# A decode step of two attention and two gated feed-forward layers: one PSUM bank of scores for a group's 4096 keys, 64 KB loads of K and V

## The chip, the cores and the metric

One of the eight cores of a Trainium2 chip runs the kernel. The metric is the device time of one execution in microseconds (us). The trace comes from one execution under the hardware profiler. TensorE's granted clock is shown in tenths of 2.4 GHz.

## The reference, cut to what matters

```python
B, Sq, D = 4, 1, 512;  Hq, Hkv, Sk, Dh = 32, 8, 4096, 128;  F = 1792      # all float32
def A(x, k_cache, v_cache, wq, wo):             # k_cache, v_cache: [B, Hkv, Sk, Dh]
    q = (x @ wq).reshape(B, Sq, Hq, Dh).transpose(0, 2, 1, 3)
    k, v = repeat(k_cache, 4, axis=1), repeat(v_cache, 4, axis=1)
    p = softmax(einsum("bhqd,bhkd->bhqk", q, k) * Dh ** -0.5)
    return einsum("bhqk,bhkd->bhqd", p, v).transpose(0, 2, 1, 3).reshape(B, Sq, Hq * Dh) @ wo
def Bff(x, w1, w3, w2):
    return (silu(x @ w1) * (x @ w3)) @ w2
for _ in range(2):                              # both layers use the same caches and weights
    x = x + A(layernorm(x), k_cache, v_cache, wq, wo)
    x = x + Bff(layernorm(x), w1, w3, w2)
```

K and V are 67.1 MB each and are needed in both layers; the buffer on the chip holds a small part of them.

## The kernel before

Everything streams from the device's memory on one queue, that of SyncE (SP). A host step lays the arrays out so that each load is 128 partitions by one contiguous row. Sizes are given per partition: 1 KB is 131,072 bytes.

Work goes by group: one of the 8 K/V heads, with its 4 query heads and all 4 batch rows. A group's 4096 keys are done in 4 steps of 1024 keys (SC). A step's K is one 16 KB row per partition and so is its V; `cache` (L92) splits some into 8 and 4 KB loads near the start and at the layers' ends. `score` (L292) makes two PSUM tiles of scores in 256-column products, four at a time, one for each batch row in its 32 output partitions. `maximum` (L312) keeps a running maximum over the steps and `sums` (L334) and the ends of `weigh` (L348) rescale the running sums (an online softmax). `turn` (L326) transposes the exponents, 128 columns at a time, and `weigh` multiplies them with V in 128-column products with 4 weight columns each. The steps are software-pipelined: `finish` (L447) of one step runs behind `score` of the next. x is kept as rows of a [128, 128] tile and is transposed for each projection (`layernorm`, L240). `busy` (L225) issues filler transposes on TensorE at eight places outside the attention steps; their counts stand in BUSY.

The order of the loads is written out in `plan` (L121 to L146). `pump` (L150) issues the next loads as long as `take` finds contiguous room; `done` and `vacate` give room back when the last product that needs a load has been issued, and pump again. So SP waits, load by load, for the products that free its room. There are three homes: the pool (96 KB), wq_sb (64 KB) and wo_sb (56 KB); in layer 1 the room of wq and wo is given to the stream as their groups are used. Layer 1 goes through the groups in reverse. K of group 7 (TURN), which ends layer 0, stays for layer 1: 60 KB in the pool and the last 4 KB in two PSUM banks (`stored`), from where ScalarE copies it back. wo's first group has no home of its own and is loaded in each layer.

Of the kernel before, what the change touches and what calls it, by code (L numbers as in the profile page):

```python
# [28 lines left out]
POOL = 96  # L29


TURN = HKV - 1
STORED = (STEPS - 1, 3)
W2_PARTS = ((0, 4), (4, 8), (8, 12), (12, 13), (13, 14))
BUSY = (5, 3, 5, 3, 3, 7, 3, 4)
SCRATCH = 1024

# [3 lines left out]
def tile_decode_layers(ctx: ExitStack, tc: tile.TileContext, x, kt, v, wq, wo, w1, w3, w2, out):  # L43
# [17 lines left out]

    homes = {"pool": pool, "wq": wq_sb.rearrange("p g k n -> p (g k n)"),
             "wo": wo_sb.rearrange("p g h e -> p (g h e)")}
    free = [("pool", 0, POOL)]

    def take(n):
        for i, (home, at, size) in enumerate(free):
            if size >= n:
                free[i:i + 1] = [(home, at + n, size - n)] if size > n else []
                return home, at, n  # L70
        return None

    def give(home, at, n):
        for other in list(free):
            if other[0] == home and other[1] + other[2] == at:
                free.remove(other)
                at, n = other[1], other[2] + n
            elif other[0] == home and at + n == other[1]:
                free.remove(other)
                n += other[2]  # L80
        free.append((home, at, n))

# [3 lines left out]
    def stream(keys, src):  # L86
        plan.append((keys, src, None))

    def keep(dst, src):
        plan.append((None, src, dst))  # L90

    def cache(which, layer, i, g, c):  # L92
        src = (kt if which == "k" else v)[g, c]
        last = i == len(orders[layer]) - 1
        if which == "k" and (g, c) == (TURN, STORED[0]):
            parts = (2, 1, 1)
        elif last:
            parts = (2, 1, 1)
        elif layer == 0 and i == 0:
            parts = (1, 1, 2)  # L100
        elif which == "v" and ((layer == 0 and i >= len(orders[0]) - 3) or (layer and i < 2)):
            parts = (2, 2)
        else:
            parts = (4,)
        r = 0
        for n in parts:
            keys = [(which, layer, g, c, r + j) for j in range(n)]
            if which == "k" and g == TURN and layer:
                if (c, r) == STORED:
                    stream(keys, None)  # L110
            else:
                stream(keys, src[:, r * U:(r + n) * U])
            r += n

    def wq_load(a, b):
        keep(wq_sb[:, a:b].rearrange("p g k n -> p (g k n)"), wq[:, a * 2 * U:b * 2 * U])

    def wo_load(a, b):
        keep(wo_sb[:, a - 1:b - 1].rearrange("p g h e -> p (g h e)"), wo[:, a * 2 * U:b * 2 * U])

    for layer in range(LAYERS):  # L121
        steps = orders[layer]
        if layer == 0:
            wq_load(0, 1)
        for i, (g, c) in enumerate(steps):
            cache("k", layer, i, g, c)
            if layer == 0 and c == 1 and g in (0, 1, 3, 5):
                wq_load(*{0: (1, 2), 1: (2, 4), 3: (4, 6), 5: (6, 8)}[g])
            if i:
                cache("v", layer, i - 1, *steps[i - 1])  # L130
            if layer == 0 and c == 2:
                if g == 0:
                    stream([("wo", 0)], wo[:, 0:2 * U])
                elif g in (1, 3, 5):
                    wo_load(g, g + 2)
        cache("v", layer, len(steps) - 1, *steps[-1])
        if layer == 0:
            wo_load(TURN, HKV)
        else:
            stream([("wo", 1)], wo[:, 0:2 * U])  # L140
        for name, w in (("w1", w1), ("w3", w3)):
            for k in range(KC):
                stream([(name, layer, k)], w[:, k * F:(k + 1) * F])
        for i, (a, b) in enumerate(W2_PARTS):
            stream([("w2", layer, i)], w2[:, a * D:b * D])

    state = {"next": 0}
    where, left, room = {}, {}, {}

    def pump():  # L150
        while state["next"] < len(plan):
            keys, src, dst = plan[state["next"]]
            if keys is None:
                nc.sync.dma_start(dst, src)
            else:
                width = U if src is None else src.shape[-1]
                got = take(width // KB)
                if got is None:
                    return
                dst = homes[got[0]][:, got[1] * KB:got[1] * KB + width]  # L160
                if src is None:
                    for i in range(2):
                        nc.scalar.activation(dst[:, i * U // 2:(i + 1) * U // 2], stored[i], AF.Copy)
                else:
                    nc.sync.dma_start(dst, src)
                n = width // len(keys)
                left[state["next"]] = len(keys)
                room[state["next"]] = got
                for i, key in enumerate(keys):
                    where[key] = dst[:, i * n:(i + 1) * n], state["next"]  # L170
                    if key[:3] == ("k", 0, TURN) and key[3:] != STORED:
                        where["k", 1, *key[2:]] = where[key]
                        kept.add(key)
            state["next"] += 1

    kept = set()

    def loaded(*key):
        return where[key][0]

    def done(*key):
        if key in kept:
            return
        i = where[key][1]
        left[i] -= 1
        if left[i] == 0:
            give(*room[i])
            pump()

    def vacate(home, at, n):  # L190
        give(home, at, n)
        pump()

    x_sb = const.tile([P, P], F32, name="x_sb")
    nc.scalar.dma_start(x_sb, x)
    pump()

# [3 lines left out]
    same = const.tile([P, 32], F32, name="same")  # L201
    nc.vector.tensor_reduce(same, ident.rearrange("p (k c) -> p c k", k=4), axis=AX.X, op=ALU.add)
    nc.vector.tensor_scalar(same, same, 1.0 / D, None, op0=ALU.mult)
    spare = const.tile([P, 1], F32, name="spare")
    half = const.tile([P, 1], F32, name="half")
    nc.vector.memset(half, -0.5)
    qT = const.tile([P, B, 32], F32, name="qT")
    nc.vector.memset(qT, 0.0)
    oT = const.tile([P, REP, B], F32, name="oT")
    hT = const.tile([P, 14, B], F32, name="hT")  # L210
    sums_ps = psum.tile([P, 2, P], F32, name="sums_ps")
    nc.vector.memset(sums_ps, 0.0)
# [314 lines left out]
```

## Time and profile before

| | |
|---|---|
| median of 3 runs | 727.63 us (726.88 to 729.59) |
| span of the profiled execution, first to last instruction | 725.7 us |
| what lies around the span, against the median | 1.9 us |
| TensorE, VectorE, ScalarE busy | 474.8, 195.1, 120.2 us |
| moved by DMA | 301.20 MB, 415 GB/s over the span |
| mean granted TensorE clock | 0.882 |

The page gives no time of the profiled execution apart from its span, so the span is what a sum is made against. Busy shares are means over the whole span; the page's rows of 40 slices (18.1 us each) show when something was busy. In a timeline each row is a start, a duration, an engine and a line; `x8` merges eight instructions. A float32 product is two MATMUL instructions with a weight load each, a transpose is one. A DMA row is the time that SP needs to issue it, not its transfer.

### The profile page before, as it was taken

How to read it: one execution, taken by the hardware profiler on the slowest of the kernel's cores; microseconds unless marked ns; L12 is line 12 of the kernel's file. 1: busy time of each engine (PE TensorE's matmuls, PEld its weight loads, DVE VectorE, ACT ScalarE, POOL GpSimd, SP SyncE). 2: the span in 40 equal slices, each digit the busy share in tenths (PEclk: the TensorE clock that was granted, in tenths of full speed). 3: DMA queues.
4: the chain of work that ended last, by engine and by line, in shares of the span. 5: the costliest groups of instructions: out<-in, count | busy, mean ns of one | idle time of the engine just before them, and what ended most of it. 6: DMA issues, size and time to landing. Idle time of an engine off the chain costs nothing.

```text
span 725.7 us, 18239 instructions
## 1 busy us (share of the span) xinstructions
PE 474.8 (65%) x8246; PEld 298.8 (41%) x8246; DVE 195.1 (27%) x694; ACT 120.2 (17%) x323; POOL 2.9 (0%) x10
## 2 busy tenths in 40 slices
PE   5664576744766556666667885666766657666687
PEld 3342344523444334444425554444444434443444
DVE  2122123221323113223202342223222233222220
ACT  1111111111111111111310221111111111111120
POOL 0000000000000000000000000000000000000000
PEclk9687878888988679999989999898989998998788
DMA  9999999999999999999989999999999999999995
GB/s 364 429 426 425 426 427 426 425 427 427 427 424 426 430 425 426 425 426 419 416 356 391 378 429 424 428 427 425 425 426 427 425 427 426 426 426 424 417 418 228
DMA packets 25853, 301.20 MB, mean 415 GB/s; under 512 B 2864, under 2 KB 3120, under 8 KB 7216
## 3 DMA queue, kind: packets, MB, share of 16 engines
q1 hardware_dynamic: 25632, 299.97, 98.4%
q8 instruction: 65, 1.06, 0.6%
q14 instruction: 12, 0.10, 0.0%
q10 hardware_dynamic: 144, 0.07, 0.0%
HBM read 299.96 MB, written 0.07 MB: 413 GB/s over the span
## 4 chain that ended last, share of the span: by engine, by line
DMA 86%; PE 12%; DVE 1%; issue 1%; SPq 0%; ACT 0%; ACTq 0%; DVEq 0%
DMA pool<-in_v 45%; DMA pool<-in_kt 21%; DMA wo_sb<-in_v 6%; DMA wq_sb<-in_v 5%; PE sums_ps L353 4%; DMA pool<-in_w 4%; PE scores L303 3%; DMA pool<-in_wo 2%; DMA wo_sb<-in_w 2%; PE turned L329 1%; PE scores L229 1%; PE scores L396 1%; PE sums_ps L425 1%; DVE stat L306 0%; PE misc L269 0%
## 5 line engine op out<-in xcount | busy, mean ns | idle before, releaser
L353 PE MATMUL sums_ps<-pool,pT 128*4 128x128 f32 x3552 | 143.1, 303 | 132.2 <-DMA pool<-in_v 107.6
L353 PEld LDWEIGHTS sums_ps<-pool,pT 128*4 128x4 f32 x3552 | 91.5, 93 | 171.2 <-issue 101.2
L303 PE MATMUL scores<-pool,qT 128*32 128x256 f32 x1760 | 118.3, 413 | 58.2 <-DMA pool<-in_kt 52.7
L323 ACT ACTIVATE p<-scores,stat 128x512 f32<-128x512 f32 x128 | 87.0, 680 | 270.9 <-PE turned L329 210.7
L306 DVE TENSOR_REDUCE stat<-scores 128x1 f32<-128x512 f32 x128 | 88.5, 691 | 135.2 <-PE scores L303 135.2
L303 PEld LDWEIGHTS scores<-pool,qT 128*32 128x32 f32 x1760 | 62.2, 117 | 97.1 <-issue 68.5
L329 PE MATMUL turned<-ident,p 128*128 128x128 f32 x512 | 96.2, 317 | 0.0
L331 DVE COPY pT<-turned 128x64 f32<-128x64 f32 x128 | 28.1, 220 | 239.2 <-PE turned L329 238.8
L329 PEld LDWEIGHTS turned<-ident,p 128*128 128x128 f32 x512 | 61.8, 157 | 47.3 <-issue 45.6
L318 ACT ACTIVATE stat<-stat 128x1 f32<-128x1 f32 x48 | 14.1, 295 | 266.0 <-DVE stat L316 266.0
L269 PE MATMUL misc<-wq_sb,xT 128*32 128x128 f32 x512 | 25.2, 302 | 0.7 <-DVE ve L258 0.4
L323 ACT ACTIVATION_READ_ACCUMULATOR p<-scores,stat 128x1 f32 x128 | 24.5, 192 | 0.0
L229 PE MATMUL scores<-ident 128*128 128x128 f32 x104 | 19.2, 315 | 1.4 <-POOL ident masks.py:199 1.4
L380 PE MATMUL sums_ps<-wo_sb,oT 128*4 128x128 f32 x448 | 15.6, 282 | 6.1 <-DVE o L362 5.4
L353 PE MATMUL sums_ps<-wq_sb,pT 128*4 128x128 f32 x320 | 11.9, 288 | 9.3 <-DMA wq_sb<-in_v 7.7
L269 PEld LDWEIGHTS misc<-wq_sb,xT 128*32 128x32 f32 x512 | 17.0, 123 | 1.5 <-ACT xT L251 0.4
L303 PE MATMUL scores<-wq_sb,qT 128*32 128x256 f32 x176 | 14.0, 466 | 3.5 <-DMA wq_sb<-in_kt 3.5
L353 PE MATMUL sums_ps<-wo_sb,pT 128*4 128x128 f32 x224 | 10.1, 337 | 9.3 <-DMA wo_sb<-in_v 8.1
L229 PEld LDWEIGHTS scores<-ident 128*128 128x128 f32 x104 | 12.9, 158 | 7.3 <-issue 5.3
L380 PEld LDWEIGHTS sums_ps<-wo_sb,oT 128*4 128x4 f32 x448 | 10.8, 88 | 11.3 <-DVE o L362 9.8
L364 DVE SCALAR_TENSOR_TENSOR o<-o,stat,sums_ps 128x128 f32<-128x128 f32 x32 | 11.0, 343 | 15.5 <-PE sums_ps L353 15.5
L396 PE MATMUL scores<-pool,xT 128*32 128x448 f32 x64 | 9.8, 700 | 5.6 <-DMA pool<-in_w 5.6
(81 smaller groups left out, 185.3 us busy)
## 6 DMA issues: line engine op xcount, KB each, us to landing
pool<-in_kt SPq DMA_DIRECT2D x49, 2048.0 KB, 29.5
pool<-in_v SPq DMA_DIRECT2D x49, 2048.0 KB, 29.3
pool<-in_v SPq DMA_DIRECT2D x10, 1024.0 KB, 14.6
wq_sb<-in_kt SPq DMA_DIRECT2D x5, 2048.0 KB, 37.7
wq_sb<-in_v SPq DMA_DIRECT2D x5, 2048.0 KB, 39.1
pool<-in_w SPq DMA_DIRECT2D x8, 896.0 KB, 9.0
wq_sb<-in_w SPq DMA_DIRECT2D x7, 896.0 KB, 17.1
wq_sb<-in_wq SPq DMA_DIRECT2D x3, 2048.0 KB, 32.5
```

The source lines that it names most:

```text
L229: nc.tensor.transpose(pt[:, 0:P], ident, ident)
L269: nc.tensor.matmul(pq[32 * h:32 * h + 32, 0, :], xT[:, 32 * k:32 * k + 32], wq_sb[:, g, k, h * DH:(h + 1) * DH], start=(k == 0), stop=(k = ...
L303: nc.tensor.matmul(ps[32 * b:32 * b + 32, r * QC:(r + 1) * QC], qT[:, b, :], t[:, b, :], start=True, stop=True)
L306: nc.vector.tensor_reduce(st["stat"][:, h:h + 1], ps, axis=AX.X, op=ALU.max, negate=True)
L318: nc.scalar.activation(stat[:, 6:7], stat[:, 2:3], AF.Exp, bias=stat[:, 3:4], scale=-1.0)
L323: nc.scalar.activation(st["p"].rearrange("p n s -> p (n s)"), st["ps"][h], AF.Exp, bias=stat[:, 3:4], accum_out=stat[:, 4 + h:5 + h])
L329: nc.tensor.transpose(pt[:, n, :], st["p"][:, n, :], ident)
L331: nc.vector.tensor_copy(pT, pt.rearrange("p n (b h) -> p n b h", b=B)[:, :, :, 0:REP])
L353: nc.tensor.matmul(o_ps[32 * b:32 * b + REP, :], st["pT"][h][:, NT * (r % 2) + n, b, :], t[:, b, n, :], start=(r == 0 and n == 0), stop=(r ...
L364: nc.vector.scalar_tensor_tensor(acc["o"], acc["o"], st["stat"][:, 6:7], o_ps, op0=ALU.mult, op1=ALU.add)
L380: nc.tensor.matmul(x_ps[32 * k:32 * k + B, :], oT[:, h, :], w[:, h, k * P:(k + 1) * P], start=(h == 0), stop=(h == REP - 1))
L396: nc.tensor.matmul(ps[32 * j:32 * j + 32, 0:FJ], xT[:, 32 * k:32 * k + 32], w[:, j * FJ:(j + 1) * FJ], start=(k == 0), stop=(k == KC - 1))
```

## The change

A group's K is one load of 64 KB per partition and so is its V. `scores` accumulates all 8 blocks of 512 keys into one PSUM bank: the query sits in a padded tile (`qpad`), and a block's products take the 32 columns of it in which the group's four heads stand in the rows of that block, so that row 4 blk + h of a batch row's 32 holds head h of block blk. One maximum, one exponent, and a factor for each row (in `softmax`: two 32-by-32 transposes on VectorE, a few small operations and an exponent) take the place of the running maximum. `weigh` multiplies four blocks of V side by side (512 columns) with all 32 rows and picks the matching parts with `sel`. x is kept turned (`xT`, [128, 4, 4]), so projections need no transpose ahead of them, and their outputs are turned back by products with a selection matrix (`rows`). The filler transposes are gone. One arena of 213 KB has wq at 0 to 64, wo at 64 to 128 and the kept V of group 7 at 128 to 192 (all K and V streams use 64 to 213 in layer 0). wo is loaded once, after the last V of layer 0, and all its products with layer 0's outputs follow there.

```diff
+NB = 8;  BK = SK // NB;  NI = BK // P;  GW = SK * B;  WT = 14;  ARENA = 213        # KB = 256 columns
+    WQ, WO, KEPT = 0, 64, 128
+    free = [(WO, ARENA - WO)]                        # take: first fit; a load at < WO has its own place
+    load(wq[:, 0:8 * KB], 8, [("wq", 0, 0)], WQ)     # a load: source, KB per key, keys, place
+    for n in range(HKV):
+        cache("k", 0, n, (32, 32) if n == 0 else (64,))
+        if n == 0:
+            load(wq[:, 8 * KB:64 * KB], 8, [("wq", 0, g) for g in range(1, HKV)], WQ + 8)
+        else:
+            cache("v", 0, n - 1, (64,))
+    cache("v", 0, TURN, (32, 16, 8, 8))              # at KEPT; not loaded again in layer 1
+    weights("wo", wo, 0, (32, 16, 8, 8), 8, WO)
+    for name, w in (("w1", w1), ("w3", w3)):
+        weights(name, w, 0, (7, 7, 7, 7), 7)
+    weights("w2", w2, 0, (6, 6, 6, 6, 2, 2), 2)
+    cache("k", 1, TURN, (8,) * 8)
+    for n in range(1, HKV):
+        cache("k", 1, order[1][n], (16,) * 4 if n == 1 else (64,))
+        if n > 1:
+            cache("v", 1, order[1][n - 1], (64,))
+    cache("v", 1, 0, (32, 16, 16))
+    for name, w in (("w1", w1), ("w3", w3)):
+        weights(name, w, 1, (28,), 7)
+    weights("w2", w2, 1, (16, 8, 2, 2), 2)
...
+    def project_q(layer, g, rq, ps):
+        w = loaded("wq", 0, g).rearrange("p (k n) -> p k n", k=KC)
         for k in range(KC):
+            nc.tensor.matmul(ps[32 * k:32 * k + 32, :], xc[:, k, :], w[:, k, :], start=True, stop=True)
+        if layer:
+            vacate("wq", 0, g)
+        yield
+        nc.vector.tensor_scalar(t, ps, rq(), None, op0=ALU.mult)
+        m = misc()
+        for h in range(REP):
+            nc.tensor.matmul(m[:, h, :], t[:, h * P:(h + 1) * P], rows[:, 0:B], start=True, stop=True)
+        nc.vector.tensor_copy(qT[:, g], m)
+        yield
+    def scores(layer, g, pieces=iter(())):
+        for blk in range(NB):
+            k = loaded("k", layer, g, blk).rearrange("p (b s) -> p b s", b=B)
+            lo = PAD - REP * blk
+            for b in range(B):
+                nc.tensor.matmul(s_ps[32 * b:32 * b + 32, :], qpad[:, b, lo:lo + 32], k[:, b, :],
+                                 start=(blk == 0), stop=(blk == NB - 1))
+            done("k", layer, g, blk)
+            next(pieces, None)
+    def softmax():
+        nc.vector.tensor_reduce(top[:, 0:1], s_ps, axis=AX.X, op=ALU.max, negate=True)
+        l = small("l")
+        nc.scalar.activation(p, s_ps, AF.Exp, bias=top[:, 0:1], accum_out=l)
...
+        return {"parts": parts, "sums": sums}
+    def turn_p(st):
+        for i in range(NI):
+            nc.tensor.transpose(t_ps[:, i, :], p[:, i * P:(i + 1) * P], ident)
+        nc.vector.tensor_copy(pT.rearrange("p i r -> p (i r)"), t_ps.rearrange("p i r -> p (i r)"))
+        m = total(st["sums"])
...
+    def weigh(layer, g, st, pieces=iter(())):
+        for f in range(2):
+            for i in range(NI):
+                key = ("v", 0 if g == TURN else layer, g, NI * f + i)
+                w = loaded(*key).rearrange("p (b n) -> p b n", b=B)
+                for b in range(B):
+                    nc.tensor.matmul(o_ps[32 * b:32 * b + 32, :], pT[:, i, 32 * b:32 * b + 32], w[:, b, :],
+                                     start=(i == 0), stop=(i == NI - 1))
+                if g != TURN or layer:
+                    done(*key)
+                yield
+            next(pieces, None)
+            if f == 0:
+                nc.scalar.activation(t, o_ps, AF.Copy, scale=st["parts"][:, 0:1])
+            else:
+                nc.vector.scalar_tensor_tensor(t, o_ps, st["parts"][:, 1:2], t, op0=ALU.mult, op1=ALU.add)
+        m = misc()
+        for j in range(4):
+            nc.tensor.matmul(flat(m), t[:, j * P:(j + 1) * P], sel[:, j].rearrange("p h b -> p (h b)"),
+                             start=(j == 0), stop=(j == 3))
+        nc.vector.tensor_tensor(oT[:, g].rearrange("p h b -> p (h b)"), flat(m), st["r"], op=ALU.mult)
+    def project_o(layer, g, first, last):            # 4 products of 512 columns; layer 1 vacates wo's group
...
+    def collect():
+        nc.vector.tensor_copy(t, x_ps)
+        m = misc()
+        for k in range(KC):
+            nc.tensor.matmul(m[:, k, :], t[:, k * P:(k + 1) * P], rows[:, 0:B], start=True, stop=True)
+        nc.vector.tensor_tensor(xT, xT, m, op=ALU.add)
...
+    def rest_of(qs):
+        for i in range(1, HKV):
+            run(qs[i])
+            if i + 2 < HKV:
+                next(qs[i + 2])
+            yield
...
+        center()                                     # mean by one product with 1/512, then subtract
+        banks = (q_ps, o_ps, t_ps.rearrange("p i r -> p (i r)")) if layer else (q_ps,)
+        for q in qs[:len(banks)]:
+            next(q)
+        nc.vector.tensor_scalar(scale["q"], deviation(), SCALE, None, op0=ALU.mult)
+        run(qs[0])
+        place_q(steps[0])
+        for n, g in enumerate(steps):
+            if layer == 0:
+                scores(layer, g)
+                ahead = qs[n + 1] if n + 1 < HKV else iter(())
+                next(ahead, None)
+                st = softmax()
+                if before is not None:
+                    run(weigh(layer, *before, ahead))
+                run(ahead)
+            else:
+                if n == 0:
+                    scores(layer, g, rest_of(qs))
+                elif n == 1:
+                    heavy = weigh(layer, *before)
+                    scores(layer, g, zip(heavy, heavy))
+                    run(heavy)
+                else:
+                    scores(layer, g)
+                st = softmax()
+                if n > 1:
+                    run(weigh(layer, *before))
+                if n:
+                    project_o(layer, before[0], n == 1, False)
+            if n + 1 < HKV:
+                place_q(steps[n + 1])
+            turn_p(st)
+            before = (g, st)
```

The feed-forward keeps its products (448 columns for w1 and w3); w2 is 14 products of 512 columns in layer 0 and 56 of 128 in layer 1, where x itself is added by four more products into the same bank.

## Rows read from the trace of the kernel before

**Rows 1.** The page: shares, slices, DMA totals.
```profile
PE 474.8 (65%) x8246; PEld 298.8 (41%) x8246; DVE 195.1 (27%) x694; ACT 120.2 (17%) x323; POOL 2.9 (0%) x10
...
PEclk9687878888988679999989999898989998998788
...
GB/s 364 429 426 425 426 427 426 425 427 427 427 424 426 430 425 426 425 426 419 416 356 391 378 429 424 428 427 425 425 426 427 425 427 426 426 426 424 417 418 228
DMA packets 25853, 301.20 MB, mean 415 GB/s; under 512 B 2864, under 2 KB 3120, under 8 KB 7216
...
q1 hardware_dynamic: 25632, 299.97, 98.4%
q8 instruction: 65, 1.06, 0.6%
```

**Rows 2.** The page: the chain that ended last, by engine.
```profile
DMA 86%; PE 12%; DVE 1%; issue 1%; SPq 0%; ACT 0%; ACTq 0%; DVEq 0%
```

**Rows 3.** Timeline of SP in layer 1: start, us, issues.
```profile
513.19 0.33 SPq L165 DMA_DIRECT2D wo_sb<-in_kt  x1
518.08 0.33 SPq L165 DMA_DIRECT2D pool<-in_v  x1
522.97 0.33 SPq L165 DMA_DIRECT2D pool<-in_kt  x1
527.86 0.33 SPq L165 DMA_DIRECT2D pool<-in_v  x1
533.27 0.33 SPq L165 DMA_DIRECT2D pool<-in_kt  x1
...
646.77 0.33 SPq L165 DMA_DIRECT2D wq_sb<-in_kt  x1
```

**Rows 4.** Timeline, layer 0's feed-forward: w1's last, w3's last, w2's first products.
```profile
371.35 0.96 PE L396 MATMUL scores<-pool,xT 128*32 128x448 f32 x8 [1.20 <-DMA pool<-in_w]
...
380.05 1.72 PE L396 MATMUL scores<-pool,xT 128*32 128x448 f32 x8 [0.42 <-DMA pool<-in_w]
...
383.86 1.06 PE L425 MATMUL sums_ps<-pool,hT 128*4 128x128 f32 x32
```

**Rows 5.** Windows: busy times, granted clock (PEclk), DMA share, GB/s.
```profile
core 0: us, PE busy (x) PEld busy (x) DVE busy (x) ACT busy (x) POOL busy (x), PEclk, DMA share, GB/s
376.00:377.00 1.00, 1.00 (x8) 0.00 (x0) 0.00 (x0) 0.00 (x0) 0.00 (x0) 0.50 0.96 401
413.00:680.00 267.00, 181.90 (x3326) 118.19 (x3318) 80.34 (x284) 46.68 (x132) 0.00 (x0) 0.90 1.01 426
```

**Rows 6.** Chain of waits: 16 score products of 256 columns.
```profile
42.11 3.68 PE scores L303 x32
...
406.06 1.77 PE scores L303 x32
```

**Rows 7.** Timeline: weight loads of transposes.
```profile
342.17 0.43 PEld L329 LDWEIGHTS turned<-ident,p 128*128 128x128 f32 x4 [0.41 <-issue]
...
715.54 0.66 PEld L411 LDWEIGHTS turned<-ident,gate 128*128 128x128 f32 x3
```

**Rows 8.** Groups by form.
```profile
L306 DVE TENSOR_REDUCE stat<-scores 128x1 f32<-128x512 f32 x128 | 88.5, 691 | 135.2 <-PE scores L303 135.2
L323 ACT ACTIVATE p<-scores,stat 128x512 f32<-128x512 f32 x128 | 87.0, 680 | 270.9 <-PE turned L329 210.7 <-issue 48.0 <-DVE stat L316 12.3
...
L269 PE MATMUL misc<-wq_sb,xT 128*32 128x128 f32 x512 | 25.2, 302 | 0.7 <-DVE ve L258 0.4 <-issue 0.3
...
L260 POOL TENSOR_TENSOR rstd<-ve,half 128x1 f32<-128x1 f32 x4 | 2.2, 550 | 698.8 <-DVE ve L258 698.8
```

**Rows 9.** The end: timeline, windows, DMA issues.
```profile
712.55 1.72 PE L396 MATMUL scores<-wo_sb,xT 128*32 128x448 f32 x8 [0.43 <-DMA wo_sb<-in_w]
...
722.73 0.29 DVE L429 SCALAR_TENSOR_TENSOR x_sb<-sums_ps,x_sb 128x128 f32<-128x128 f32 x1 [5.21 <-PE sums_ps L425]
...
723.06 0.35 SPq L487 DMA_DIRECT2D out<-x_sb  x1
...
714.00:715.00 1.00, 1.00 (x8) 0.80 (x5) 0.66 (x1) 0.00 (x0) 0.00 (x0) 0.50 0.75 307
720.00:721.00 1.00, 1.00 (x24) 0.82 (x28) 0.00 (x0) 0.00 (x0) 0.00 (x0) 1.00 0.18 53
721.00:722.00 1.00, 1.00 (x24) 0.65 (x15) 0.00 (x0) 0.00 (x0) 0.00 (x0) 1.00 0.00 0
...
out<-x_sb SPq DMA_DIRECT2D x1, 64.0 KB, 1.5
```

More of the change, by code (lines that the diff above doesn't have):

```diff
@@ L62, in tile_decode_layers @@
[L62 to L70, printed above, removed]
-        return None
[L73 to L81, printed above, removed]
@@ L84, in tile_decode_layers @@
-    plan = []
[L86 to L104, printed above, removed]
+    arena = const.tile([P, ARENA * KB], F32, name="arena")
@@ L105, in cache, with load @@
+    plan = []
+    def load(src, per, keys, at=None):
+        plan.append((src, per, keys, at))
+    def cache(which, layer, g, parts):
+        src = (kt if which == "k" else v)[g]
         r = 0
         for n in parts:
[L107 to L112, printed above, removed]
@@ new lines, in cache, with weights @@
+            at = KEPT + r if which == "v" and layer == 0 and g == TURN else None
+            load(src[:, r * KB:(r + n) * KB], 8, [(which, layer, g, r // 8 + j) for j in range(n // 8)], at)
+            r += n
+    def weights(name, src, layer, parts, per, at=None):
+        r = 0
+        for n in parts:
+            load(src[:, r * KB:(r + n) * KB], per, [(name, layer, r // per + j) for j in range(n // per)],
+                 None if at is None else at + r)
+            r += n
+    order = [list(range(HKV)), list(reversed(range(HKV)))]
@@ L147, in tile_decode_layers @@
+    cache("k", 1, TURN, (8,) * 8)
[7 more added lines that the diff above has]
+    weights("w2", w2, 1, (16, 8, 2, 2), 2)
     state = {"next": 0}
-    where, left, room = {}, {}, {}
+    where, left = {}, {}
     def pump():
         while state["next"] < len(plan):
[L152 to L173, printed above, removed]
@@ L174, in pump @@
+            src, per, keys, at = plan[state["next"]]
+            n = src.shape[-1] // KB
+            a = take(n, at)
+            if a is None:
+                return
+            nc.sync.dma_start(arena[:, a * KB:(a + n) * KB], src)
+            i = state["next"]
+            left[i] = (len(keys), a, n)
+            for j, key in enumerate(keys):
+                where[key] = (a + j * per, per, i)
             state["next"] += 1
-    kept = set()
     def loaded(*key):
-        return where[key][0]
+        a, n, _ = where[key]
@@ L429, in feed_forward @@
-        nc.vector.scalar_tensor_tensor(x_sb, x_ps, 1.0, x_sb, op0=ALU.mult, op1=ALU.add,
-                                       accum_out=rowsum)
-    def all_of(pieces):
+            nc.vector.tensor_copy(hT[64 * u:64 * u + 64, 12:14, :], rest[64 * u:64 * u + 64, :, u, 0:B])
+        if layer < LAYERS - 1:
+            for m in range(WT):
+                q = m % 4
+                nc.tensor.matmul(x_ps[32 * q:32 * q + B, :], hT[:, m, :], loaded("w2", layer, m),
+                                 start=(m < 4), stop=(m >= WT - 4))
+                done("w2", layer, m)
+            return
@@ L433, in all_of, with run @@
+        for k in range(KC):
+            nc.tensor.matmul(x_ps[32 * k:32 * k + B, 0:P], xT[:, k, :], ident, start=True, stop=False)
+        for m in range(WT):
+            w = loaded("w2", layer, m)
+            for k in range(KC):
+                nc.tensor.matmul(x_ps[32 * k:32 * k + B, 0:P], hT[:, m, :], w[:, k * P:(k + 1) * P],
+                                 start=False, stop=(m == WT - 1))
+            done("w2", layer, m)
+    def run(pieces):
         for _ in pieces:
             pass
-    rowsum = small("rowsum")
```

449 lines of the change are left out of this document (157 added, 292 removed).

## The prediction

> **What bounds the kernel now.** I read the page's busy shares and the 40 slices first, then the chain of waits, then single loads and instructions. The slices show the DMA engines full at 424 to 430 GB/s nearly throughout, the exceptions being the first slice, slices 19 to 23 (the turn from layer 0 to layer 1) and the last three; TensorE is busy 65% [rows 1]. The chain is 86% DMA [rows 2]. So the time is bytes times the price of a byte, plus what the queue loses at the start, at the turn and after the last landing.
>
> Sizes below are KB per partition (1 KB is 131,072 bytes). Before moves 2288 KB: 299.97 MB [rows 1]. In layer 1 SP issues one 16 KB load each time one lands: mostly 4.89 us apart, but (646.77 - 513.19)/27 = 4.947 on average [rows 3]. That is 0.3092 us per KB, and 2288 x 0.3092 = 707.4. The last w3 load, used at 712.55, is followed by 28 KB of w2 at 0.31, so the last byte lands at 721.2, where the windows show the engines falling empty [rows 9]. Its engines do not finish together, so I count landings. 721.2 - 707.4 = 13.8: about 3.3 is the start (the first slice's missing GB/s is 2.7, plus a landing), and 10.5 is lost at the turn. From 721.2 to the end is 4.5.
>
> **The change, part by part.**
>
> *Bytes.* After moves K 16 x 64, V 15 x 64 (layer 1 reuses the kept group), wq 64, wo 64, w1 to w3 2 x 84: 2280 KB, 8 fewer (wo's first group is loaded once). 8 x 0.3092 = -2.5.
>
> *Instructions.* fp32 products are two instructions here (the 256 products of the q projections are 512 [rows 8]). After has 704 products and 37 turns in layer 0, 746 and 37 in layer 1: 2974 matmuls and as many weight loads against 8246 each, with the other engines about 6,700 instructions against 18,239. Instruction fetch takes 1.06 MB and 0.6% of the engines [rows 1]. The excess of 4.947 over 4.89 is 0.0036 us per KB; I take it as fetch, of which 0.37 stays, 0.0013. Gain 0.0023 x 2280 = 5.2; bounds 1.6 (0.63 of 1.06 MB at 426 GB/s) and 5.2; fetching less can't cost time.
>
> *Rows of 64 KB.* w1 and w3 come in 7 KB rows: (380.05 - 371.35)/4 = 2.175 us each [rows 4], 0.311 per KB against 0.3056 for 16 KB. A line through both, 0.063 + 0.3017 per KB, gives 19.37 us for 64 KB, 0.3027 per KB: (0.3056 - 0.3027) x 2280 = 6.6. Bounds: 0 (the overhead belongs to pieces that a 64 KB row is cut into anyway) and 6.6; I take 6.6, since the profile counts one packet a row for both sizes (25,632 on the queue, about what rows and completions add up to). Together 0.3040 per KB, 693.1 in all, 14.3 less than before.
> A rule speaks against this. wq and wo are read before already in slices whose rows lie 64 KB apart, nine loads in the first 18 slices, and from the second on these stay at 424 to 430 [rows 1]. The Trainium skill ("DMA: Bandwidth & Descriptors", section "Latency and other measured facts") gives a lower rate where rows lie a large power of two apart, about 3% at 512 KB; by it K and V, whose rows now lie 64 KB apart, could run some 21 us longer, an estimate from that page. The rows show none of it, so it is a rival.
>
> *Inside a layer.* In layer 0 only 149 KB of the buffer is free for streams, so two slots: a K load issues when all scores of the last group are done, a V load when its products are. A 512-column group of four products costs twice a 256-column one, 1.77/4 x 2 = 0.88 us at 2.4 GHz and 3.68/4 x 2 = 1.84 at half that [rows 6]; eight of them are 7.0 or 14.7. Scores free the slot 0.65 (landing) + 7.0 to 14.7 + 1.0 (semaphore, SP's issue, start) = 8.7 to 16.4 us after the last byte; the other slot's load covers 19.4. For V add 0.9 for the ScalarE copy between halves [rows 8]: up to 17.3. I cost the softmax, the online maximum's removal and all 512-column work at 0; the cover is the 19.4 us. Were it gone, each us would count 27 times. The 0.65 and 0.85 around a transfer are my split of the 1.5 us of the 64 KB store [rows 9].
>
> *The turn.* Here the buffers are small: wq, wo and the kept V hold 192 KB, so w1, w3, w2 and the first K go through 21 KB. Weight loads of 128 columns: 0.43/4 = 0.11 at 2.4 GHz, 0.66/3 = 0.22 at 1.2 [rows 7]; four fp32 products with such weights are eight, 0.9 to 2.0 with the tail. The filler products that kept TensorE busy are gone; after 20 us of sparse work I take 1.2 GHz (it falls to 0.50 already in today's feed-forward [rows 5]).
> 1. After wo's last byte the queue has 21 KB of w1, 6.5 us. Chain to the first release: landing 0.65, project_o 1.9, copy 0.8, four turned products 2.0, add 0.2, mean 0.7, subtract 0.5, w1 group 1.7, restart 1.0 = 9.4. Idle 2.9.
> 2. w1, w3 stream. After w3's last byte 18 KB of w2 cover 5.6; the fourth part waits for w2's first: 0.65, then 380.05 to 383.86 = 3.8 today, 4.0 taken [rows 4], group 1.4, restart 1.0 = 7.05. Idle 1.5.
> 3. After w2's last byte 16 KB of K cover 4.95; more needs wq to be freed by layer 1's first projection: 0.65 + group 1.2 + copy 0.8 + turned 1.8 + add 0.2 + mean and subtract 1.1 + projection 1.6 + restart 1.0 = 8.35. Idle 3.4.
> 4. Three freed wq slots cover 7.4. Next slot: first K block scored. Two projections 2.8, variance, power and scale 2.1 (GpSimd's power 0.55 [rows 8]), scaling 0.75, turning 1.8, copies 0.45, scores 1.3 = 9.2. Idle 1.8, and 1.0 more at the first 16 KB of the next K.
> 5. The next K after that (64 KB) needs a whole 64 KB slot, and the only one is where the kept V lies: it waits until the last product with it. From the first scored block: five pieces of turn 1.35 + projection 0.88 + scores 0.88 = 3.1, two of 2.2, softmax and turn_p 3.5 (0.69 reduce + 0.68 exponent + turns and copy [rows 8]), then 4 score and 8 V groups 12 x 0.88 = 10.6 and 1.0 of half clock: 35.0. Loads in that time: 88 KB = 27.0, and the 1.0 idle already counted. Idle 7.0.
> Sum 17.6 against 10.5: +7.1. Ends: all at 2.4 GHz about 12; all at 1.2 about 45.
>
> *The end.* w3 lands as one 28 KB load 36.5 + 0.65 after V's last load starts; its products meet a slow TensorE: 5.2; then multiply 0.9, turns 1.2, copies 0.4, w2 14 x 0.25 = 3.5, copy 0.3, store and rest 2.7 [rows 9]: 51.4, of which 45.1 is transfer. So 5.65 from the last landing on against 4.5: +1.2; ends -1 (2.4 GHz) and +3.
>
> Sum on the profiled execution: 725.7 - 14.3 + 7.1 + 1.2 = 719.7. The runs' median, 727.63, is 1.9 above the span; the same on top gives 721.6.
>
> **Rivals.**
> A. The byte is no cheaper in longer rows: 721.6 + 6.6 = 728.2; with the lower bound for the instructions too (+3.6): 731.8. For it: nothing in the trace shows a row above 16 KB. Against: the two sizes it shows differ by 1.7%.
> B, slower. The kept V holds the only large slot, and TensorE, with no fillers, stays at 1.2 GHz through stall 5. Then pieces of 6.0 and 4.2, 12 x 1.84, 4.5: 65 us instead of 35.0, up to +30: 751.6; half of it 737. It decides the sign once that stretch runs beyond 41 us. For it: the clock fell in today's feed-forward [rows 5]. Against: that stretch is dense, and dense stretches of layer 1 run at 0.90 on average [rows 5]. The Trainium skill ("TensorE: Matmul & The Clock Gate", section "HAM oscillation — how this bites in real kernels") says that waits on DMA between bursts put the clock back to half; by that rule the groups in the layers start slow as well, which their cover hides.
> C. Rows 64 KB apart cost bandwidth, 3% on 1984 KB: +18, 740. Against: [rows 1], above.
> D. The turn is as fast as today (idle 10.5): 714.5. For it: only 8 KB less and a queue that restarts in 1 us; against: 21 KB of room.
>
> **How the numbers follow.** Forecast 0.45 (its own range 716 to 727: the turn's idle 12 to 23), A 0.27, B 0.15, C 0.05, D 0.08. About 0.5% is what a measurement here can tell from no change: 724.0 and 731.3. Faster: 0.36 of the forecast, 0.02 of A, all of D: 0.46. Same: 0.09 of it, 0.19 of A, 0.02 of B: 0.30. Slower: 0.06 of A, 0.13 of B, C: 0.24. The range 714 to 738 leaves out most of C, the upper half of B and a little of D, under 2 in 10.
>
> **What would show it.** Right: 64 KB loads 19.4 to 19.5 us apart in layer 1; GB/s above 428 in full slices; under 0.3% of the engines for instructions; five dips at the turn, the longest before the second 64 KB K of layer 1 and ended by the V products; five to six us from last landing to end. Wrong: loads 19.7 us or more apart (A), 20 or more (C); idle DMA between loads inside a layer (the cover is gone); granted clock 0.5 through layer 1's first scores (B).

## The result, and the profile after

The changed kernel takes 730.19 us (median of 14 runs), the kernel before 727.84 on the same chip: ratio 1.0028, 95% interval 1.0016 to 1.0039. That is slower by 0.28%. The forecast was 721.6, 0.8% faster; its range, 714 to 738, holds the time, but the time went the other way. The profiled execution spans 728.2 us, against 725.7.

The page of the changed kernel, to be read beside [rows 1, 2]:
```profile
PE 423.2 (58%) x2982; PEld 146.2 (20%) x2982; DVE 87.5 (12%) x285; ACT 35.2 (5%) x75; POOL 2.9 (0%) x10
...
PEclk9857777877777777668657699678786867877798
...
GB/s 382 439 444 450 415 454 408 454 408 454 422 437 428 433 432 429 437 408 427 297 325 282 310 380 367 407 455 410 455 410 451 414 447 419 443 426 436 415 432 304
DMA packets 10827, 299.33 MB, mean 411 GB/s; under 512 B 1328, under 2 KB 1456, under 8 KB 3504
...
q1 hardware_dynamic: 10656, 298.91, 96.4%
q8 instruction: 23, 0.38, 0.2%
...
DMA 64%; PE 29%; another core or an unknown queue 3%; DVE 1%; ACT 1%; issue 1%; SPq 0%; POOL 0%; DVEq 0%; POOLq 0%
```
Full slices now average 432 GB/s instead of 426, and the instruction queue is down to 0.2%: the transfers did become cheaper. Slices 20 to 26 gave it back (counted from 1, as in the prediction). Where before three slices read 356 to 391 [rows 1], six now read 282 to 380, and TensorE has risen to 29% of the chain, from 12% [rows 2].

Windows of the changed kernel: a stretch inside layer 0, the turn as a whole, the turn in its five stalls and what follows, the first microseconds after wo landed, and the end (columns: us, busy time of PE, PEld, DVE, ACT, POOL, granted clock, DMA share, GB/s):
```profile
20.00:340.00 320.00, 175.66 (x1228) 60.83 (x1220) 36.17 (x108) 14.82 (x34) 0.00 (x0) 0.75 1.00 432
355.00:444.00 89.00, 69.66 (x431) 25.73 (x431) 15.74 (x50) 3.79 (x7) 1.10 (x2) 0.75 0.78 300
...
355.00:366.00 11.00, 9.11 (x44) 3.92 (x44) 1.72 (x8) 0.00 (x0) 0.55 (x1) 0.53 0.52 185
366.00:386.00 20.00, 10.99 (x59) 2.19 (x57) 1.81 (x5) 2.12 (x3) 0.00 (x0) 0.58 0.89 323
386.00:396.00 10.00, 5.98 (x38) 1.77 (x36) 1.29 (x5) 0.00 (x0) 0.00 (x0) 0.99 0.90 344
396.00:404.00 8.00, 5.87 (x33) 2.30 (x34) 1.34 (x6) 0.00 (x0) 0.55 (x1) 0.74 0.70 261
404.00:416.00 12.00, 11.52 (x54) 5.23 (x58) 2.67 (x7) 0.00 (x0) 0.00 (x0) 0.50 0.84 315
416.00:422.00 6.00, 6.00 (x52) 2.69 (x48) 1.66 (x4) 0.00 (x0) 0.00 (x0) 0.92 0.49 161
422.00:440.00 18.00, 16.19 (x142) 6.58 (x138) 4.63 (x16) 1.67 (x4) 0.00 (x0) 1.00 1.01 430
440.00:447.00 7.00, 6.92 (x68) 2.63 (x64) 0.93 (x2) 0.00 (x0) 0.00 (x0) 1.00 0.52 176
...
356.00:357.00 1.00, 0.71 (x4) 0.00 (x0) 0.25 (x1) 0.00 (x0) 0.00 (x0) 0.50 0.95 394
357.00:358.00 1.00, 0.50 (x3) 0.50 (x3) 0.44 (x1) 0.00 (x0) 0.00 (x0) 0.50 0.92 380
358.00:359.00 1.00, 1.00 (x6) 1.00 (x7) 0.00 (x0) 0.00 (x0) 0.00 (x0) 0.50 0.55 229
359.00:360.00 1.00, 0.74 (x4) 0.65 (x4) 0.17 (x1) 0.00 (x0) 0.00 (x0) 0.50 0.23 93
...
722.00:724.00 2.00, 1.62 (x64) 1.29 (x56) 0.00 (x0) 0.00 (x0) 0.00 (x0) 1.00 0.62 236
724.00:726.00 2.00, 1.09 (x36) 0.50 (x24) 0.29 (x1) 0.00 (x0) 0.00 (x0) 1.00 0.01 5
```
A stretch's loss is its length times (1 - GB/s / 432). The turn loses 89 x (1 - 300/432) = 27.2 us up to 444. The forecast had 17.6. The table gives it stall by stall (windows that end at 366, 386, 404, 422 and 447), beside the same sum for an experiment told below (to 364.5, 382, 398, 426 and 440). The last window ends where the next row starts, because the profile counts a 64 KB row whole at its start: from 444 to 445 it reads 1049 GB/s, in the two microseconds after it 0.

| stall | forecast | changed kernel | e9 (clock held up) |
|---|---|---|---|
| 1, behind wo | 2.9 | 6.3 | 4.7 |
| 2, w1 and w3 | 1.5 | 5.0 | 2.4 |
| 3, behind w2, first projection | 3.4 | 5.2 | 3.5 |
| 4, first K blocks | 2.8 | 7.0 | 1.6 |
| 5, the kept V's place | 7.0 | 4.2 | 5.9 |
| sum | 17.6 | 27.7 | 18.1 |

Timeline of the changed kernel's feed-forward (start us, us, engine, what, [idle before, released by]):
```profile
363.25 5.96 SPq L118 DMA_DIRECT2D arena<-in_w  x4
...
367.86 0.96 PE L324 MATMUL s_ps<-arena,xc 128*32 128x448 f32 x8 [1.81 <-DMA arena<-in_w]
371.40 1.72 PE L324 MATMUL o_ps<-arena,xc 128*32 128x448 f32 x8 [2.58 <-DMA arena<-in_w]
374.14 1.72 PE L324 MATMUL o_ps<-arena,xc 128*32 128x448 f32 x8 [1.01 <-DMA arena<-in_w]
376.33 1.72 PE L324 MATMUL o_ps<-arena,xc 128*32 128x448 f32 x8 [0.47 <-DMA arena<-in_w]
380.05 1.72 PE L324 MATMUL o_ps<-arena,xc 128*32 128x448 f32 x8 [2.00 <-DMA arena<-in_w]
...
406.69 1.87 PE L237 MATMUL m_ps<-rows,t 128*128 128x4 f32 x8
408.49 1.94 PE L230 MATMUL q_ps<-arena,xc 128*32 128x512 f32 x8
410.20 1.94 PE L249 MATMUL s_ps<-arena,qpad 128*32 128x512 f32 x8
412.07 1.87 PE L237 MATMUL m_ps<-rows,t 128*128 128x4 f32 x8
```
Three things are to be seen. The load issued at 363.25 is used at 367.86: 4.61 us for 7 KB, whose transfer is 2.18 where such loads follow one another [rows 4], so 2.43 beside it, where I had 0.65 + 0.85. Landings lie 2.2 to 3.7 apart, not 2.18. And a piece in layer 1's first scores (turned products, a projection and a scored block) takes 5.4 us (406.69 to 412.07) at half clock, although PE is busy for 11.52 of the 12 us from 404 to 416.

### The profile page after: what moved, and what is told of

The parts are those of the page before. It is cut to its first block, busy times and chain, and to the rows that moved or that the text cites. A ratio compares the mean times of both kernels' runs of the same rounds, so it can differ in the third digit from the quotient of the medians.

```text
span 728.2 us, 6611 instructions
## 1 busy us (share of the span) xinstructions
PE 423.2 (58%) x2982; PEld 146.2 (20%) x2982; DVE 87.5 (12%) x285; ACT 35.2 (5%) x75; POOL 2.9 (0%) x10
## 2 busy tenths in 40 slices
DMA packets 10827, 299.33 MB, mean 411 GB/s; under 512 B 1328, under 2 KB 1456, under 8 KB 3504
## 4 chain that ended last, share of the span: by engine, by line
DMA 64%; PE 29%; another core or an unknown queue 3%; DVE 1%; ACT 1%; issue 1%; SPq 0%; POOL 0%; DVEq 0%; POOLq 0%
DMA arena<-in_v 47%; PE o_ps L289 18%; DMA arena<-in_w 8%; DMA arena<-in_wq 5%; DMA arena<-in_wo 4%; PE s_ps L249 3%; PE m_ps L237 2%; ACT t L296 1%; PE q_ps L230 1%; PE o_ps L230 1%; PE x_ps L347 1%; PE o_ps L324 0%; PE s_ps L324 0%; PE m_ps L316 0%
## 5 line engine op out<-in xcount | busy, mean ns | idle before, releaser
L289 PE MATMUL o_ps<-arena,pT 128*32 128x512 f32 x1024 | 146.9, 724 | 140.9 <-DMA arena<-in_v 127.6
L249 PE MATMUL s_ps<-arena,qpad 128*32 128x512 f32 x1024 | 150.9, 745 | 92.9 <-DMA arena<-in_kt 92.4
L289 PEld LDWEIGHTS o_ps<-arena,pT 128*32 128x32 f32 x1024 | 37.4, 130 | 242.6 <-issue 218.8
L249 PEld LDWEIGHTS s_ps<-arena,qpad 128*32 128x32 f32 x1024 | 40.1, 133 | 185.6 <-issue 180.7
L301 PE MATMUL m_ps<-sel,t 128*128 128x16 f32 x128 | 17.0, 265 | 14.2 <-DVE t L298 14.1
L237 PE MATMUL m_ps<-rows,t 128*128 128x4 f32 x128 | 20.6, 284 | 5.1 <-DVE t L234 5.1
L237 PEld LDWEIGHTS m_ps<-rows,t 128*128 128x128 f32 x128 | 19.2, 230 | 20.8 <-issue 13.0
L308 PE MATMUL x_ps<-arena,oT 128*4 128x512 f32 x128 | 18.0, 669 | 8.9 <-DMA arena<-in_wo 7.0
L230 PE MATMUL q_ps<-arena,xc 128*32 128x512 f32 x88 | 14.6, 738 | 12.9 <-DMA arena<-in_wq 11.9
L301 PEld LDWEIGHTS m_ps<-sel,t 128*128 128x128 f32 x128 | 15.5, 191 | 28.8 <-DVE t L298 28.8
```

What stands on the lines that cost most here:

```text
L230: nc.tensor.matmul(ps[32 * k:32 * k + 32, :], xc[:, k, :], w[:, k, :], start=True, stop=True)
L237: nc.tensor.matmul(m[:, h, :], t[:, h * P:(h + 1) * P], rows[:, 0:B], start=True, stop=True)
L249: nc.tensor.matmul(s_ps[32 * b:32 * b + 32, :], qpad[:, b, lo:lo + 32], k[:, b, :], start=(blk == 0), stop=(blk == NB - 1))
L289: nc.tensor.matmul(o_ps[32 * b:32 * b + 32, :], pT[:, i, 32 * b:32 * b + 32], w[:, b, :], start=(i == 0), stop=(i == NI - 1))
L301: nc.tensor.matmul(flat(m), t[:, j * P:(j + 1) * P], sel[:, j].rearrange("p h b -> p (h b)"), start=(j == 0), stop=(j == 3))
L308: nc.tensor.matmul(x_ps[32 * h:32 * h + B, :], oT[:, g, h, :], w[:, h, :], start=first, stop=last)
```

## The experiments

Ratios are to the kernel before; the changed kernel stands at 1.0028. Theory T: too little room and a longer round trip, that is, the time from a load's issue to its use. Theory C: TensorE's clock. The wait for the kept V's place is a third. GB/s from 355 to 444 us measures the turn.

**e1, rows of 16 KB inside the layers.**
```diff
-        cache("k", 0, n, (32, 32) if n == 0 else (64,))
+        cache("k", 0, n, (32, 32) if n == 0 else (16,) * 4, None if n == 0 else 128)
-            cache("v", 0, n - 1, (64,))
+            cache("v", 0, n - 1, (16,) * 4, 64)
```
and the same for layer 1's from the fourth K and third V on.


> The changed kernel with 24 of its 64 KB loads (1536 KB of 2280: those inside the layers, none near the turn) taken as four loads of 16 KB each into the same places. Longer rows are cheaper (the prediction's term): a K and V pair then lands 39.1 us apart (8 x 4.89) instead of 38.70, and the time is (39.1 - 38.7) x 12 = 4.9 us above the changed kernel's, about 735, ratio to before 1.009 to 1.010. Rival, only the fewer instructions made the byte cheaper: pairs stay 38.7 to 38.8 apart and the time stays at about 730, ratio 1.002 to 1.004.


1.0110 (1.0088 to 1.0132), 735.42 us. The timeline of e1, uses of a V that ended a wait, one group apart; the same in the changed kernel; and e1's window:
```profile
82.53 3.46 PE L289 MATMUL o_ps<-arena,pT 128*32 128x512 f32 x16 [2.86 <-DMA arena<-in_v]
...
121.70 1.92 PE L289 MATMUL o_ps<-arena,pT 128*32 128x512 f32 x16 [1.35 <-DMA arena<-in_v]
```
```profile
198.32 5.41 PE L289 MATMUL o_ps<-arena,pT 128*32 128x512 f32 x32 [8.51 <-DMA arena<-in_v]
237.01 6.54 PE L289 MATMUL o_ps<-arena,pT 128*32 128x512 f32 x32 [9.08 <-DMA arena<-in_v]
```
```profile
20.00:340.00 320.00, 204.07 (x1223) 60.03 (x1212) 35.43 (x107) 14.83 (x34) 0.00 (x0) 0.76 1.01 428
```
A K and a V are 39.17 apart instead of 38.69. Longer rows are cheaper: 128 KB save 0.48, the rows' term is shown. Row and load grew together, so the two are not told apart. What e1 keeps above the kernel before inside a layer (428 against the 426 of [rows 5]) fits the fewer instructions, which were not tried alone; its 16 KB rows lie 64 KB apart, and it shows no loss by that.

**e2, filler products over the turn; e5, the same with fewer.**
```diff
+    def fill(n):
+        for _ in range(n):
+            nc.tensor.matmul(pad[0:32, :], ident[:, 0:32], one.broadcast_to([P, 512]), start=True, stop=True)
...
+                fill({0: 16, 4: 4, 7: 5}.get(g, 0))
                 project_o(layer, g, g == 0, g == HKV - 1)
```
with others after the parts of w1, w3 and w2 and ahead of the first turned q.


> The changed kernel with filler products (four-instruction-free of data, 512 columns, into a PSUM bank of their own) in TensorE's waits from wo's landing to layer 1's first turned q. Theory C, the clock is the cause of the turn's extra idle: the granted clock reads 1.00 from 345 to 430, the groups of w1 and w3 take 0.96 us instead of 1.72, so that their slots come free in 2.18 + 2.45 + 0.96 = 5.6 us and the 7 KB loads land 2.2 to 2.4 apart again; the first three q pieces take 2.9 instead of 5.5 each. The turn's idle falls from 27 to 17 to 20 us and the time by 7 to 10, to 720 to 723, ratio 0.990 to 0.994. Theory T, room and round trip are the cause whatever the clock: loads of w1 and w3 still land 2.5 to 3.7 apart and the time falls by 0 to 3, 727 to 730, ratio 0.999 to 1.003.


1.0419 (1.0395 to 1.0443), 758.49 us: neither. The timeline of e2, the 16 fillers ahead of wo's products:
```profile
339.75 13.55 PE L191 MATMUL pad<-few,ident 128*32 128x512 f32 x31
```
That is 0.85 us a filler at a granted clock of 1.00 (340 to 352), where I had counted 0.22, a quarter of the 0.88 that four products side by side take [rows 6]. The 0.43 in the next expectation is one of a filler's two instructions. So the fillers held up the products that free the slots, and e2 tells nothing of T or C.


> As e2_fill, but with fillers that fit the waits: each took 0.43 us there, not 0.22 as planned, so 10, 3 and 3 among wo's products instead of 16, 4 and 5, 5 after the third part of w1, 2 or 1 after the later parts, 4 before the first turned q. Room stays 21 KB. Theory C (clock): the granted clock is 1.00 from 345 to 430 and the time falls by 7 to 10 under the changed kernel's 730.2, ratio to before 0.990 to 0.994. Theory T (room and round trip): the loads of w1 and w3 still land 2.3 to 3.7 apart, since a slot is refilled only 2.45 + 2.18 + 0.96 us after its last landing at the earliest, the q pieces save part of their 8 us, and the time falls by 2 to 5, ratio 0.996 to 1.000.


1.0005 (0.9990 to 1.0020), 728.33. This is at the upper end of T's range, but the fillers stood in wo's way still: its first product ran at 347.50 instead of 345.19.

**e9, fillers that fit.** Against e5, cut:
```diff
-                fill({0: 10, 4: 3, 7: 3}.get(g, 0))
+                fill({0: 5, 7: 1}.get(g, 0))
-        product("w1", s_ps, (0, 0, 5, 2))
+        product("w1", s_ps, (0, 0, 3, 2))
```


> e5_fill2 with fewer fillers where they stood in wo's way: its products after wo's last byte ran 3.8 us later than the changed kernel's (the first of each 32 KB part waited behind fillers at half clock). Five ahead of wo's products instead of 10, none between, one before the last; three instead of five in w1. Room stays 21 KB. If the clock is a second term of the miss beside the room, the time falls by 3.8 more than e5_fill2's 2, to 723 to 725, ratio 0.994 to 0.997; if the chains wait for landings whatever the clock, it stays at 727 to 729, ratio 0.999 to 1.002. In neither case does it come near e4_keep32's 716.


0.9914 (0.9900 to 0.9929), 721.0 us: better than either number, 1.1% below the changed kernel with the same room and loads. Timeline and window of e9:
```profile
369.60 0.96 PE L334 MATMUL o_ps<-arena,xc 128*32 128x448 f32 x8 [0.61 <-DMA arena<-in_w]
...
371.90 1.10 PE L334 MATMUL o_ps<-arena,xc 128*32 128x448 f32 x8
...
374.15 1.33 PE L334 MATMUL o_ps<-arena,xc 128*32 128x448 f32 x8
...
376.33 0.58 PE L334 MATMUL o_ps<-arena,xc 128*32 128x448 f32 x3
```
```profile
355.00:364.50 9.50, 8.36 (x49) 3.44 (x50) 1.72 (x8) 0.00 (x0) 0.55 (x1) 0.82 0.59 217
364.50:382.00 17.50, 16.43 (x80) 4.16 (x78) 1.81 (x5) 2.12 (x3) 0.00 (x0) 1.00 0.99 372
382.00:390.00 8.00, 5.96 (x33) 2.00 (x30) 0.86 (x2) 0.00 (x0) 0.00 (x0) 1.00 0.99 387
390.00:398.00 8.00, 7.52 (x43) 2.60 (x43) 1.77 (x8) 0.00 (x0) 0.55 (x1) 1.00 0.75 288
398.00:409.00 11.00, 10.53 (x90) 5.24 (x89) 3.50 (x9) 0.00 (x0) 0.00 (x0) 1.00 1.00 387
409.00:426.00 17.00, 15.40 (x113) 6.71 (x116) 5.55 (x17) 0.98 (x3) 0.00 (x0) 0.80 1.01 420
426.00:436.00 10.00, 9.91 (x92) 3.31 (x88) 0.93 (x2) 0.69 (x1) 0.00 (x0) 1.00 0.63 238
436.00:440.00 4.00, 3.17 (x31) 0.77 (x22) 1.52 (x5) 0.81 (x3) 0.00 (x0) 1.00 0.65 279
```
With the clock at 1.00 w3's parts come 2.2 to 2.3 apart, and the turn loses 18.1. T alone has fallen: at 21 KB of room the clock is worth about 8 us. C alone does not explain the turn either: 18.1 us are still lost with the clock at 0.94 on average from 355 to 444.

**e3, the third K of layer 1 in four parts.**
```diff
-        cache("k", 1, order[1][n], (16,) * 4 if n == 1 else (64,))
+        cache("k", 1, order[1][n], (16,) * 4 if n <= 2 else ((32, 32) if n == 3 else (64,)))
-            cache("v", 1, order[1][n - 1], (64,))
+            cache("v", 1, order[1][n - 1], (32, 32) if n == 2 else (64,))
```


> The changed kernel with layer 1's third K (group 5) loaded in four parts of 16 KB and the next V and K in halves, so that they go into the small freed slots of wq and need not wait for the 64 KB of the kept V. If the wait for that slot costs the 4.2 us in which the DMA engines stood empty (440.3 to 444.5), the time falls by 3.5 to 4.5 to about 726, ratio 0.997 to 0.998, and no window from 430 to 470 reads under 390 GB/s. Rival, the load after it becomes late instead, because the products with the kept V release everything behind it: 0 to -1.5, 729 to 730, ratio 1.001 to 1.003.


0.9972 (0.9951 to 0.9992), 725.0. As expected of the wait for the kept V's place.

**e12, e9 and e3 together.** The two edits above.


> e9_fill4 and e3_k5 together, at 21 KB of room: TensorE kept at 2.4 GHz over the turn, and layer 1's third K in parts that need not wait for the kept V's place. If the clock (9 us) and the wait for that place (4 to 5 us) are separate terms of the turn's idle, they add up: 716 to 717.5, ratio 0.984 to 0.987. If the faster chain had taken the wait away already, or makes the next load late, 719.5 to 721.5, ratio 0.989 to 0.992.


0.9861 (0.9843 to 0.9879), 717.5. This is in the range of two terms that add up.

**e4, half of the last V kept; e6, with fillers.** In e4 the third K and the V behind it also come in halves, much as in e3, so that the wait for the kept V's place shrinks too.
```diff
+    part("k", TURN - 1, 0, (16, 16))
+    part("v", TURN, 32, (16, 16))
+    part("k", TURN - 1, 32, (16, 16))
...
-                key = ("v", 0 if g == TURN else layer, g, NI * f + i)
+                key = ("v", 0 if g == TURN and f == 0 else layer, g, NI * f + i)
-                if g != TURN or layer:
+                if g != TURN or layer or f:
```


> The changed kernel that keeps only half of layer 0's last V (32 KB instead of 64) and loads the other half again in layer 1 (before the second half of that layer's second K); the 32 KB go to the weights at the turn. It adds 32 x 0.3024 = 9.7 us of transfer. Theory T (21 KB of room is the cause): with 53 KB of room every chain of the turn (8 to 10 us) lies under queued loads of 15 us, w1 and w3 land 2.18 apart, the turn's idle falls from 27 to 5 to 9, and the time falls by 8 to 12, to 718 to 722, ratio 0.987 to 0.992, though the granted clock still reads 0.5 in the feed-forward. Theory C (the clock): the idle stays at 20 or more and the time rises by 3 to 10, to 733 to 740, ratio 1.007 to 1.017.


0.9838 (0.9816 to 0.9860), 716.1 us, with 4.2 MB more to move. Timeline and window of e4:
```profile
366.01 0.96 PE L333 MATMUL o_ps<-arena,xc 128*32 128x448 f32 x8 [1.20 <-DMA arena<-in_w]
368.20 0.96 PE L333 MATMUL o_ps<-arena,xc 128*32 128x448 f32 x8 [1.23 <-DMA arena<-in_w]
370.39 0.96 PE L333 MATMUL o_ps<-arena,xc 128*32 128x448 f32 x8 [1.23 <-DMA arena<-in_w]
```
```profile
355.00:444.00 89.00, 71.82 (x481) 27.63 (x485) 18.91 (x61) 4.77 (x10) 1.10 (x2) 0.83 0.99 410
```
Loads are 2.19 apart and the turn loses 89 x (1 - 410/432) = 4.5.


> e4_keep32 with the fitting fillers (none where a load sets the wait of w1's first parts, none in w2). With 53 KB of room all chains but one are covered: what e4 still lost at the turn stood at 390 to 420, about 3.6 us by its windows, with the first q pieces at half clock. Theory T with the clock as its second term: the fillers take back 1 to 3 of them, 713 to 715, ratio 0.980 to 0.983. Rival, the fillers delay the products that free the slots: 0 to +3, 716 to 719, ratio 0.984 to 0.989.


0.9858 (0.9830 to 0.9886), 717.44: not the gain that I expected, but the rival's range. Its window:
```profile
355.00:444.00 89.00, 79.98 (x545) 29.55 (x544) 18.90 (x61) 4.77 (x10) 1.10 (x2) 0.95 1.00 414
```
The clock rose from 0.83 to 0.95 and the time did not fall. e6 does not price the clock at 53 KB, though: it has e5's fillers, and its last products with wo start at 359.84, e4's at 355.21, which is the delay that the rival names. What it could have gained is bounded by the 4.5 that e4's turn loses.

**e8, the kernel before with less room.** `POOL = 96` becomes `POOL = 81`.


> The kernel before, with 81 KB instead of 96 in the pool through which it streams, so that 21 KB instead of 36 are left beside the 60 KB that it keeps over the turn. Its fillers stay. Theory T (room): each chain of the turn has 4.6 us less of queued loads above it, the idle of its turn rises from 10.5 to 17 to 25, the time by 6 to 15, ratio 1.009 to 1.021. Theory C (clock): the fillers keep TensorE at 2.4 GHz as before, 0 to +2, ratio 1.000 to 1.003. A gain of 5 us or more inside the layers is not expected by either.


1.0250 (1.0226 to 1.0275), 746.09: above T's range. Its page:
```profile
GB/s 366 429 427 427 425 427 426 424 430 424 427 426 426 426 428 426 424 425 358 283 287 288 317 430 424 428 425 427 424 429 424 425 428 424 428 424 427 417 417 237
```
Hardly anything changed but slices 19 to 23. So the kernel before, with 36 KB and 8,246 products, also lived off its room. Its fillers did not hold the clock up with 21 KB (0.84 from 345 to 440, against 0.96 with 36 KB), so e8 does not part room from clock.

**e7, e10, e11: 48 KB kept.** As e4, with V's last 16 KB loaded again and e3's parts; e10 makes the small parts 8 KB, the size of a slot of wq; e11 adds fillers, fewer than e9. e10 against e7:
```diff
-    part("k", TURN - 1, 0, (16, 16, 16))
-    part("v", TURN, 48, (16,))
-    part("k", TURN - 1, 48, (16,))
+    part("k", TURN - 1, 0, (8,) * 6)
+    part("v", TURN, 48, (8, 8))
+    part("k", TURN - 1, 48, (8, 8))
```


> e4_keep32 with 48 KB of the last V kept and 16 KB loaded again: 4.85 us of transfer less, 37 KB of room at the turn instead of 53, and the third K of layer 1 in four parts as in e3_k5. If 37 KB, 11.5 us of queued loads, still cover chains of 8 to 10 us, the time is 711 to 713, ratio 0.977 to 0.981. Rival, that the room of 53 KB was just enough: 16 KB less cost 4.9 us at each of two or more chains, 716 to 722, ratio 0.984 to 0.992.


0.9847 (0.9828 to 0.9865), 716.78: no faster than e4, the rival's range. A part of the transfer that it saves went into waits for 16 KB places: from 400 to 404 it moved 61 GB/s.


> e7_keep48 with layer 1's second K and the reloaded V in parts of 8 KB, the size of a freed slot of wq; in e7_keep48 they were 16 KB and waited for two slots side by side, the DMA engines all but empty from 400 to 404 (about 3.2 us). If that wait was what ate the 4.85 us of saved transfer, the time is 712.5 to 714.5, ratio 0.979 to 0.982. Rival, the wait only moves to the next 16 KB load: 715.5 to 717, ratio 0.983 to 0.986.


0.9823 (0.9799 to 0.9847), 714.32: between the two ranges.


> e10_keep48_k8 with fillers as in e9_fill4, but none in w1's first three parts and in w2. If the first q pieces at half clock still cost there, 0.5 to 2 us less than e10_keep48_k8; if the room covers them, the same within 0.5; if the fillers delay the chain, up to 2 more.


0.9799 (0.9776 to 0.9822), 712.48, the fastest measured. Its window:
```profile
355.00:444.00 89.00, 77.35 (x551) 28.45 (x555) 18.83 (x61) 4.77 (x10) 1.10 (x2) 0.98 1.01 411
```
The steps from e7 to e10 to e11 go the expected way, but neighbouring intervals overlap; e11 against e7, and its 2.0% against the kernel before, are clear.

## Why the prediction was wrong

- **Transfers: right.** Forecast -14.3. By the pages 299.33 MB at 432 GB/s are 692.9 us, 301.20 at 426 were 707.0: -14.1. The rows' share, 6.6, is shown by e1: at 0.48 per 128 KB it is 8.5 over all 2280 KB as an upper end, since not all loads are of 64 KB. For the 26 loads of 64 KB alone it is 6.2. The instructions' share was not tried alone.
- **Inside a layer: right.** DMA stands at 1.00 of the time; the cover of 19.4 us held.
- **The turn: the step that failed, in stalls 1 to 4** (10.6 forecast, 23.5 measured). The chains were named rightly; four things around them were sized wrongly. First, the round trip: "the 0.65 and 0.85 around a transfer", split from one store, are 2.43 on a small load into an idle queue. Second, the cover: behind wo the 21 KB were not worth 6.5 us after its landing. The engines fell off from 380 GB/s at 357 to 93 at 359; in the 6.5 us from 354.5, which is 0.65 before wo's last part was used, they moved 1.8 MB, not the 2.75 of 21 KB. The chain itself held: 8.1 us from that use (355.15) to the issue at 363.25, where the forecast has 7.8. Third, the loop: in stall 2 "w1, w3 stream" costed the fourth part alone and not the loop of three slots. By the numbers above that is 2.43 + 2.18 + 1.72 = 6.3 at half clock, against 3 x 2.18 = 6.5 of transfers, and leaves 0.2 for SP or a late part; with 0.96 it is 5.6. Fourth, the pieces: one priced at 3.1 took 5.4 in stall 4.
- **Clock or room?** Of the turn's loss e9 takes 9.6 back by the clock (27.7 to 18.1). e4 takes back 22.7 by room and the shorter wait for the kept V's place together (27.2 to 4.5). So neither is the cause by itself: a chain at half clock costs much only where the queue above it is short. The prediction's own figure for a turn all at 2.4 GHz was about 12; e9, near that, loses 18.1. So as an estimate about 6 of the turn's excess of 10 are round trip and cover, and the rest is more time at 1.2 GHz than forecast. No run parts them directly.
- **Stall 5: found in its place, smaller** (4.2 for 7.0). The stretch before its load was 36.5 us for a forecast 35.0, and most of stall 4's 7.0 lies inside it, so less was left. In e9, where the stalls ahead are shorter, it grows to 5.9.
- **The baseline.** I took 10.5 as the kernel before's loss at its turn. Its slices [rows 1] lose 18.1 x (1 - GB/s / 426) each, 6.9 in 20 to 23; the other 3.6 belonged to its end, where its last slice reads 228 against 304 now. The engines are empty from 724 on, 4.2 us before the end; before, from 721, 4.7 [rows 9]. So the end, forecast at +1.2, is a gain of about 3. By luck these two errors nearly cancel, and what is left is stalls 1 to 4: +20 at the turn, -3 at the end, -14 for transfers and -0.5 at the start make the +2.5 of the spans.
- **Rival B** named the right engine and mostly the wrong place: half clock held in the feed-forward and in layer 1's first pieces, up to 416, and not through stall 5 (1.00 from 422 to 446). Its stretch, from the first scored block to the K load, ran 36.5 us (406.8 to 443.3), under the 41 that it asked for. The Trainium skill ("TensorE: Matmul & The Clock Gate", section "HAM oscillation — how this bites in real kernels") has waits on DMA between bursts put the clock back; windows 355 to 386, at 0.53 and 0.58, agree. From 404 to 416 the clock read 0.50 with PE busy 11.52 of 12 us, which that sentence does not cover.
- **Rival A** and **C** fell with the 432 GB/s, A with e1 as well; **D** fell with the turn. The prediction's 21 us for C's rule took in all 2280 KB; for K and V alone it is C's own 18.

## What to carry to other kernels

Where streams stop at a layer's end, compare the queued bytes above each dependent chain with that chain at half clock, its load's whole round trip counted; kept data that saves transfer can cost more in room than it saves (with 32 KB less kept, e4 moved 4.2 MB more and ran 1.9% faster than the changed kernel). Fillers and room cover in part the same loss, so price them together: e12, which keeps all 64 KB, holds the clock up and needs no 64 KB place at once, is hardly behind e4 (0.9861 against 0.9838, with intervals that overlap). Split one loss over the stretches by GB/s before using it as a baseline.

## What the runs showed of the hardware

A 64 KB row costs less per byte than a 16 KB one (38.69 against 39.17 us per 128 KB). Rows that lie 64 KB apart ran at 432 GB/s in whole layers; the loss that the Trainium skill ("DMA: Bandwidth & Descriptors", section "Latency and other measured facts") gives for larger pitches did not appear at this one. A lone fp32 product of 512 columns, two instructions, took 0.85 us at full clock (e2's fillers), about as long as four side by side (0.88 [rows 6]).
